# Two attention and gated layers on one core: a new instruction list for the input's stretch, and other step orders for six units

## The chip, the cores and the metric

The kernel runs on one core of one Trainium2 chip. The metric is the time of one execution on the device in microseconds (us). A core has five engines that run beside each other and wait for each other on semaphores: TensorE (PE in the profile, its weight loads PEld), VectorE (DVE), ScalarE (ACT), GpSimd (POOL) and SyncE (SP), which here only issues DMAs. Each engine works through its own instructions in the order in which the program wrote them, so a waiting instruction holds up all that stand behind it on its engine.

## The reference

The input x has 2048 rows of 448. Four sublayers follow each other, attention and a gated block in turn, twice over, with the same weights in both layers:

```python
x = x + A(layernorm(x)); x = x + B(layernorm(x))      # and both once more
# A: 16 heads of 28; q = h@wq for each head, one k = h@wk and one v = h@wv for all heads
#    softmax(q k^T * 28**-0.5) v, heads side by side, @ wo
# B: (sigmoid(h@w_gate) * (h@w_up)) @ w_down, inner width 1792
```

## The kernel before, in words

Everything is float32 in and out. Most products are done on float16 operands that are split in two: a high part (the rounded value) and a low part (the rest), so one product is three matmuls (high by high, high by low, low by high).

**The layer as units.** A layer is cut into 16 units of 128 rows, and a unit into 16 steps, one for each block of 128 keys, so a layer has 256 steps. One step does the scores of its unit's rows with its keys: four matmuls `s` (line 592), each followed by an exponential on ScalarE into a tile `P` (line 595), and, a step or so later, four products `pv` of `P` with the values (line 634, or 629 for halved tiles). Beside them a step computes row maxima of the unit after, since the exponent needs them: `Maxima.step` does one of 16 groups for a unit, four small matmuls `mx` (line 557) and four reductions on VectorE (line 562). After a unit's last group `row_max` reduces and rounds the maxima, and at the next visit of the maxima it transposes them on TensorE (`mt`, line 583), copies them (`mr`, line 585) and sends them by DMA into a row of the query tile `QS` (line 586): from GpSimd's queue for units 1 to 3, from SyncE's for the others. A unit's first scores can't start before that row has landed.

**The fill.** What is left, queries of later blocks (`qp`), the output projection (`wo`), the gated block (`gp`, `up`, `dn`), is handed out by `Filler.slice` in small pieces between the scores. How much a slice does follows from the work left over the steps left.

**The step orders.** The string for a step says in which order it writes its parts: S one score matmul with its exponential, F a slice of the fill, P the products of waiting steps, M one step of the maxima, X the stages that turn a finished unit into rows of the result (`tick`), and with it the pacing of the weights. `PATHS` has a pair of strings, for even and odd steps, and `pair_of` chooses the pair by layer and unit. `MORE` gives step 15 of unit 0 a second step of the maxima. Two steps of unit 1's maxima run before step 0.

**The input's stretch.** Before unit 0 stands a list written out by hand, `SEQ`. It takes x through statistics (s), normalization (n; last number 1: ScalarE, 0: VectorE), high part (g; 1: VectorE), low part (l; 1: GpSimd, 0: VectorE; lines 996 and 997), transposition on TensorE (t, line 338, and its copy, line 340), keys and values (k, line 355 `kv`), the keys' transposition (c, lines 396 and 397), the split of the query weights `WQ` (qs, qx, qy, qw), queries (f, slices of the fill), unit 0's 16 steps of the maxima (m), and dummy matmuls on the identity that keep TensorE's clock up (h, line 954). p is one step of the preparation of the other weights, e writes out what was put off.

**The weights.** `prep_b` reads the weights of the gated block and `wo`, takes their mean squares on ScalarE (line 109) for scales, and splits them, 46 splits in all. `HOWS` deals the splits: d is ScalarE and VectorE, p is ScalarE and GpSimd (lines 135 to 137), q is GpSimd alone (lines 141 to 143). `PLAN` says after how many steps of layer 0 how many steps of the preparation must be done. The split columns go to memory (line 254) and come back as `wgu` (line 769).

Of the kernel before, what the change touches and what calls it, by code (L numbers as in the profile page):

```python
# [19 lines left out]
def interleaved_layers_kernel(ctx: ExitStack, tc: tile.TileContext, x, wq, wk, wv, wo, wg, wu, wd, out, layers=2):  # L20
# [147 lines left out]
    def prep_b():  # L168
# [26 lines left out]
        def fetch(n):  # L195
            while todo and len(raw) < n:
                fn, *args = todo.pop(0)
                raw.append(fn(*args))
# [32 lines left out]
        for c in range(4):  # L231
            SPLIT[HOWS[c]](WO[:, 0, c], WO[:, 1, c], ro[c // 2][:, c % 2], swb[:, 0:1])
            fetch(c)
# [13 lines left out]
        for f in range(FC):  # L247
            r = get()
            st = big.tile([128, 2, 2, 4, 128], F16, tag="big", name="sgu")
            for j in (1, 0):  # L250
                SPLIT[HOWS[4 + 2 * f + j]](st[:, j, 0], st[:, j, 1], r[:, j], swb[:, 1 + j:2 + j])
                if j == 0:
# [6 lines left out]
        for f in range(0, FC, 2):  # L259
            r = get()  # L260
            for j in range(2):
                SPLIT[HOWS[32 + f + j]](WD[:, f + j, 0], WD[:, f + j, 1], r[:, j], swb[:, 3:4])
            yield
# [2 lines left out]


    SPLIT = {"d": split_d, "p": split_p, "q": split_pp}
    HOWS = "pppqdpppdqdqdqdppqdppqqqpdqpdpdqddpqqdqppdqdqd"
    PLAN = [(0, 9), (26, 29), (31, 33), (63, 61), (73, 67)]  # L270
    prepd = [0]

    def paced(step):

        k = next((i for i in range(len(PLAN) - 1) if PLAN[i + 1][0] > step), None)
        if k is None:
            n = 10 ** 6
        else:
            (a, p), (b, q) = PLAN[k], PLAN[k + 1]
            n = p + (q - p) * (step + 1 - a) / (b - a)  # L280
# [760 lines left out]
    def first_mx():  # L1041
# [8 lines left out]
          "h": heat, "a": lambda: next(pkv, None), "qs": qsq, "qx": qsum, "qy": lambda: next(pws), "qw": qsplit,  # L1050
          "q": queries, "f": lambda a: fill.slice(a * QCH / 100), "p": advance, "e": flush}
    SEQ = (
# [13 lines left out]
    )  # L1066
    for o in SEQ.split():
        a = o.split(",")
        DO[a[0]](*map(int, a[1:]))
    for b in range(1, NB):  # L1070
# [1 line left out]

    fill.slice(0.4 * QCH)
    early[0] = False
    MORE = (15,)
    HEAD = U * KT - 36
    sparse = ()
    PATHS = {
        "A": ("SFFFFSFFSSFPXM", "FSSFFSXPSM"),
        "A2": ("FFSFSSFSPXM", "FSFSFSSPMX"),  # L1080
        "B0": ("FSSFSXSPPM", "SFFSSFFXMFS"),
        "B1": ("FSFSFXSFSPMP", "SSFSFFXSFM"),
        "C": ("FFSXFSSSPPM", "SFFXMFFSSFSF"),
        "C2": ("FSXFSSSPPM", "SFFXFMSFSFS"),
        "C3": ("FSFSXFSSPPM", "SSFFFXSFFMS"),
        "D0": ("FSFSXFSSPPM", "FSFFSXSFFMS"),
        "D1": ("FSFSXFSSPPM", "FSFSFXSFSFM"),
        "E0": ("FFXFSSSSPPM", "SSFFFXSFFMS"),
        "E1": ("SFSFXFSSFPPM", "SSSFFXSM"),
    }  # L1090

    def pair_of(l, u):
        if not l and u < 4:
            return PATHS["A" if u < 2 else "A2"]
        if l and u < 3:
            return PATHS["C" if u < 2 else "C2"]
        if l and u == 3:
            return PATHS["C3"]
        return PATHS[("E" if l and u > 13 else "BD"[l]) + str(u % 2)]
# [4 lines left out]
    for l in range(layers):  # L1104
# [8 lines left out]
        else:  # L1113
            mx.todo.sort()
            n = sum(a[0] < 4 for a in mx.todo) + 4
# [10 lines left out]
        for step in range(U * KT):  # L1126
            u, kt = divmod(step, KT)
            if step == HEAD and not final:
                mxs[l + 1] = Maxima(l + 1)
            P = []  # L1130
            pair = pair_of(l, u)
            single = len(pair) == 2 and "P" in pair[0] and "P" in pair[1]
            for o in pair[kt % len(pair)]:
                if o == "S":
                    scores(l, u, kt, len(P), P)
                elif o == "M":
                    if l and step < 3 * KT:
                        n = step in sparse
                    else:
                        n = 1 + (u == 0 and kt in MORE)  # L1140
                    if not n:
                        mx.visit()
                    for _ in range(n):
                        if not mx.step() and not final and l + 1 in mxs:
                            a = mxs[l + 1].between()
# [28 lines left out]
        n = 0  # L1174
        nx = None if final else mxs[l + 1]
        while side or pend or (fill.gens if final else not nx.started()):
# [4 lines left out]
            a = None if final else nx.between()  # L1181
            if a:
# [7 lines left out]
                if go:  # L1190
                    nx.step(a)
                    n = 0
# [25 lines left out]
```

## Time and profile before

| what | value |
|---|---|
| time, median of 3 runs | 2234.21 us (2233.69 to 2234.92) |
| time of the profiled execution | 2234.31 us |
| its span in the profile | 2232.5 us |
| busy in the span: TensorE, VectorE, ScalarE, GpSimd | 2181.6, 1661.5, 1652.0, 910.0 us |
| granted TensorE clock, mean | 0.995 |
| first reduction of unit 0's maxima | 35.13 us |
| first scores of unit 0, 1, 2, 3 | 91.69, 145.82, 201.09, 260.01 us |

The span runs from the first instruction to the last; the rest of the execution's time lies around it. A busy TensorE is counted by matmuls that overlap each other, so a full row says that it had matmuls in it all the time, not that they ran at the highest rate. In a group's row the number after x is the count, then come busy us, the mean ns of one, and, behind the second bar, the idle time of the engine just before these instructions with what ended it.

### The profile page before, as it was taken

How to read it: one execution, taken by the hardware profiler on the slowest of the kernel's cores; microseconds unless marked ns; L12 is line 12 of the kernel's file. 1: busy time of each engine (PE TensorE's matmuls, PEld its weight loads, DVE VectorE, ACT ScalarE, POOL GpSimd, SP SyncE). 2: the span in 40 equal slices, each digit the busy share in tenths (PEclk: the TensorE clock that was granted, in tenths of full speed). 3: DMA queues.
4: the chain of work that ended last, by engine and by line, in shares of the span. 5: the costliest groups of instructions: out<-in, count | busy, mean ns of one | idle time of the engine just before them, and what ended most of it. 6: DMA issues, size and time to landing. Idle time of an engine off the chain costs nothing.

```text
span 2232.5 us, 43041 instructions
## 1 busy us (share of the span) xinstructions
PE 2181.6 (98%) x16306; PEld 1037.2 (46%) x16306; DVE 1661.5 (74%) x2983; ACT 1652.0 (74%) x2795; POOL 910.0 (41%) x1095
## 2 busy tenths in 40 slices
PE   7899999999999999999999999999999999999999
PEld 3322344454444444454564234545454545545467
DVE  7888877767767777777786556888888888888421
ACT  5698777776667777676623997888888888888851
POOL 4123775111111111111122011577676777767751
PEclk9999999999999999999999999999999999999999
DMA  5233662423223142332341113232231323232233
GB/s 175 74 96 87 204 212 75 121 62 114 89 62 112 39 125 73 105 100 60 113 151 54 36 52 101 70 108 80 87 94 53 105 62 103 62 108 78 97 109 116
DMA packets 203632, 213.39 MB, mean 96 GB/s; under 512 B 135376, under 2 KB 164240, under 8 KB 203424
## 3 DMA queue, kind: packets, MB, share of 16 engines
q1 hardware_dynamic: 198880, 195.88, 29.6%
q0 software_dynamic: 4544, 14.77, 1.7%
q8 instruction: 127, 2.08, 0.4%
q14 instruction: 81, 0.66, 0.1%
HBM read 175.37 MB, written 23.59 MB: 89 GB/s over the span
## 4 chain that ended last, share of the span: by engine, by line
PE 86%; DVE 5%; ACT 2%; DMA 1%; issue 1%; SPq 1%; POOL 1%; DVEq 0%; ACTq 0%; POOLq 0%
PE s L592 19%; PE pv L634 16%; PE dn L822 11%; PE gp L355 11%; PE up L355 11%; PE mx L557 7%; DVE mp L562 3%; PE wo L734 3%; PE pv L629 3%; PE qp L355 2%; ACT P L595 2%; DVE PH L611 1%; DMA sums<-rc 0%; SPq L453 0%; POOL PH L612 0%
## 5 line engine op out<-in xcount | busy, mean ns | idle before, releaser
L595 ACT ACTIVATE P<-s,esc 128x512 f32<-128x512 f32 x2048 | 1299.0, 693 | 356.2 <-PE s L592 336.7
L562 DVE TENSOR_REDUCE mp<-mx 128x1 f32<-128x512 f32 x2048 | 1269.8, 684 | 365.7 <-PE mx L557 360.9
L592 PE MATMUL s<-QS,KK 96*128 96x512 f16 x2048 | 694.9, 382 | 13.4 <-DVE mp L562 8.6
L355 PEld LDWEIGHTS <-wgu 128*128 128x128 f16 x4928 | 465.6, 97 | 200.2 <-issue 52.6
L612 POOL TENSOR_TENSOR PH<-P,PH 128x512 f16<-128x512 f32 x384 | 443.0, 1178 | 132.2 <-DVE PH L611 130.8
L634 PE MATMUL pv<-P,VV 128*32 128x512 f32 x3328 | 425.5, 601 | 0.0
L355 PE MATMUL gp<-XT,wgu 128*128 128x256 f16 x2464 | 357.1, 272 | 0.5 <-ACT P L595 0.2
L355 PE MATMUL up<-XT,wgu 128*128 128x256 f16 x2464 | 354.0, 273 | 3.5 <-DVE mp L562 3.5
L797 POOL TENSOR_TENSOR h<-th,h 128x512 f16<-128x512 f32 x112 | 130.9, 1168 | 454.4 <-ACT h L796 454.4
L822 PE MATMUL dn<-WD,h 128*128 128x448 f16 x1344 | 303.2, 352 | 0.0
L592 PEld LDWEIGHTS <-KK 96*128 96x128 f16 x2048 | 191.8, 97 | 210.6 <-issue 123.1
L557 PE MATMUL mx<-KK,QH 32*128 32x512 f16 x1792 | 187.8, 384 | 7.8 <-ACT P L595 4.5
L822 PEld LDWEIGHTS <-h 128*128 128x128 f16 x1344 | 126.6, 97 | 129.8 <-issue 13.0
L557 PEld LDWEIGHTS <-QH 32*128 32x128 f16 x1792 | 46.5, 91 | 250.5 <-issue 248.1
L634 PEld LDWEIGHTS pv<-P,VV 128*32 128x32 f32 x3328 | 81.9, 109 | 162.6 <-issue 141.8
L611 DVE CAST PH<-P 128x512 f16<-128x512 f32 x192 | 106.1, 578 | 31.8 <-ACT P L595 31.7
L309 POOL TENSOR_SCALAR rs<-mv 128x1 f32<-128x1 f32 (+1 forms) x50 | 13.4, 268 | 266.4 <-DVE mv L294 264.1
L796 ACT CAST h<-th 128x512 f16<-128x512 f32 x112 | 69.2, 618 | 61.9 <-DVE th L793 61.0
L355 PE MATMUL qp<-XT,WQ 128*128 128x512 f16 x352 | 109.3, 388 | 1.0 <-DVE mp L562 0.7
L609 ACT CAST PH<-P 128x512 f16<-128x512 f32 x192 | 110.2, 633 | 0.0
L793 DVE SCALAR_TENSOR_TENSOR th<-th,up 128x512 f32<-128x512 f32 x112 | 76.2, 681 | 39.1 <-PE up L355 37.7
L785 ACT ACTIVATE th<-gp,gsc 128x512 f32<-128x512 f32 x112 | 77.2, 689 | 33.4 <-PE gp L355 33.3
(166 smaller groups left out, 1188.0 us busy)
## 6 DMA issues: line engine op xcount, KB each, us to landing
wgu<-wgu_d SPq DMA_DIRECT2D x224, 512.0 KB
QS<-qd SPq DMA_DIRECT2D x384, 32.0 KB
lb<-sums SPq DMA_DIRECT2D x128, 64.0 KB
xr<-in_A_x_dram SPq DMA_DIRECT2D x32, 224.0 KB
qd<-qst POOLq DMA_DIRECT2D x28, 256.0 KB, 2.6
wgu_d<-sgu POOLq DMA_DIRECT2D x14, 512.0 KB, 4.0
x2d<-x SPq DMA_DIRECT2D x16, 224.0 KB
xr<-x2d SPq DMA_DIRECT2D x16, 224.0 KB
```

The lines of the kernel that those rows point to most:

```text
L355: nc.tensor.matmul(ps, a, b, start=n == 0, stop=n == 10)
L557: nc.tensor.matmul(ps[h][:, i * w:(i + 1) * w], qh[32 * h:32 * h + 32, g], KK[l][32 * h:32 * h + 32, 1, ka:kz], start=True, stop=True, til ...
L562: nc.vector.tensor_reduce(o, ps[h].rearrange("p (g k) -> p g k", g=n), axis=AX.X, op=OP.max)
L592: nc.tensor.matmul(s, KK[l][0:96, 0, kt * 128:(kt + 1) * 128], QS[l, u][:, g].rearrange("p h n -> p (h n)"), start=True, stop=True)
L595: nc.scalar.activation(p, s, AF.Exp, scale=esc)
L609: nc.scalar.copy(hi, p)
L611: (nc.vector if how == "d" else nc.gpsimd).tensor_copy(hi, p)
L612: nc.gpsimd.tensor_tensor(lo, p, hi, op=OP.subtract)
L634: nc.tensor.matmul(v[32 * g:32 * g + 32], VV[l][:, kt], P[g], start=kt == 0, stop=kt == KT - 1, tile_position=(0, 32 * g))
L785: defer(lambda: nc.scalar.activation(th, gp.rearrange("p j n -> p (j n)"), AF.Tanh, scale=gsc))
L797: nc.gpsimd.tensor_tensor(h[:, 1], t, h[:, 0], op=OP.subtract)
L822: nc.tensor.matmul(p, hs[f // 2][:, a, o:o + 128], WD[:, f, c], start=n == 0, stop=n == 3 * FC - 1)
```

## The change

Four tables are changed, and two lines of code that read them.

`SEQ` is another list with the same parts: 16 statistics, normalizations, high parts, low parts, transpositions, keys, 16 steps of the maxima, 136 dummy matmuls. Fifteen low parts go to GpSimd, where nine did; one stays on VectorE, where seven were. The scale of the query weights (qx, qy) is asked for ahead of the first transpositions, and no dummies stand ahead of the first scale. `PATHS` has a pair of its own for each of units 0 to 5 of layer 0 (A0 to A5), where units 0 and 1 shared A, 2 and 3 shared A2, and 4 and 5 had B0 and B1. The second step of the maxima in step 15 (`MORE`) is gone; `EXTRA` puts one more M into step 100 (unit 6). In layer 1 the odd string of C3 (unit 3) and of D0 (units 4, 6, 8, 10, 12) and both strings of E1 (unit 15) are reordered. `HOWS` deals the splits in another order: 15 d, 19 p, 12 q, where there were 15, 16 and 15. `PLAN` has its last point at (72, 66).

```diff
-    HOWS = "pppqdpppdqdqdqdppqdppqqqpdqpdpdqddpqqdqppdqdqd"
-    PLAN = [(0, 9), (26, 29), (31, 33), (63, 61), (73, 67)]
+    HOWS = "qppddqpppddqppdpdqdddqpqdpdpppdpqpqqdpdqpdqpqp"
+    PLAN = [(0, 9), (26, 29), (31, 33), (63, 61), (72, 66)]
...
-        "h,2 h,3 s,0,2,0 e s,2,4,0 r,0 f,20 a e h,18 e h,2 n,1,0 g,1,0 qs,1 r,2 a n,0,0 n,3,0 qs,3 g,3,0 "
-        "g,0,1 l,1,0 l,0,0 t,0,0 l,3,0 h,2 n,2,0 h,2 a h,1 e qs,0 e g,2,0 h,3 qs,2 l,2,1 f,30 t,1,0 p "
+        "e a s,0,2,0 h,2 r,0 h,3 h,2 h,18 s,2,4,0 e e qs,1 a n,1,0 e h,1 g,1,1 qs,0 h,2 qs,3 r,2 n,0,0 n,3,0 "
+        "h,3 f,5 l,1,1 n,2,0 g,3,1 g,0,0 l,0,1 l,3,1 qs,2 qx g,2,0 f,100 t,0,0 l,2,1 s,4,8,1 a t,1,0 t,2,0 e "
...
-    MORE = (15,)
+    EXTRA = {100: 5}
...
-        "A": ("SFFFFSFFSSFPXM", "FSSFFSXPSM"),
-        "A2": ("FFSFSSFSPXM", "FSFSFSSPMX"),
+        "A0": ("FSFFFSFFFSSPMX", "SSFFFSXPMS"),
+        "A1": ("FSFFSFFFSSPXM", "FFSFSFSFXPSM"),
+        "A2": ("SFFFFFFSFSFFFFFSFXPMFF", "FFSSPSFFSMXF"),
+        "A3": ("FFSSFSSPMX", "FSFFSSSPMX"),
+        "A4": ("SFFXSSSPPM", "SFFFSSFFXSFMFF"),
+        "A5": ("FXFSSSPMPS", "SFSFSXSFFFMFFF"),
...
-        "C3": ("FSFSXFSSPPM", "SSFFFXSFFMS"),
-        "D0": ("FSFSXFSSPPM", "FSFFSXSFFMS"),
+        "C3": ("FSFSXFSSPPM", "SSFFSFXSFFM"),
+        "D0": ("FSFSXFSSPPM", "FSFFSSXFFMFS"),
...
-        "E1": ("SFSFXFSSFPPM", "SSSFFXSM"),
+        "E1": ("SFSFXMFSSFPP", "FSSSFFXSM"),
...
-        if not l and u < 4:
-            return PATHS["A" if u < 2 else "A2"]
+        if not l and u < 6:
+            return PATHS["A" + str(u)]
...
-            for o in pair[kt % len(pair)]:
+            path = pair[kt % len(pair)]
+            if not l and step in EXTRA:
+                path = path[:EXTRA[step]] + "M" + path[EXTRA[step]:]
+            for o in path:
...
-                        n = 1 + (u == 0 and kt in MORE)
+                        n = 1
```

Three places show what this does to the engines' own orders.

GpSimd in the input's stretch, before, from its first square roots on (rs is a tile of row statistics, hl a tile's high and low parts, xr a tile of x, WQ the query weights, ro the raw `wo`):

```order
L971 TENSOR_TENSOR rs<-rs,mhalf 128x2 x2
L996 TENSOR_TENSOR hl_274<-xr_136,hl_274 128x64
L997 TENSOR_TENSOR hl_274<-xr_136,hl_274 128x384
L207 MEMSET ro 128x896 x2
L309 TENSOR_SCALAR rs<-mv 128x4
```

The same place now:

```order
L971 TENSOR_TENSOR rs<-rs,mhalf 128x2 x2
L996 TENSOR_TENSOR hl_234<-xr_128,hl_234 128x64
L997 TENSOR_TENSOR hl_234<-xr_128,hl_234 128x384
L996 TENSOR_TENSOR hl_256<-xr_126,hl_256 128x64
L997 TENSOR_TENSOR hl_256<-xr_126,hl_256 128x384
L996 TENSOR_TENSOR hl_254<-xr_138,hl_254 128x64
L997 TENSOR_TENSOR hl_254<-xr_138,hl_254 128x384
L996 TENSOR_TENSOR hl_267<-xr_136,hl_267 128x64
L997 TENSOR_TENSOR hl_267<-xr_136,hl_267 128x384
L309 TENSOR_SCALAR rs<-mv 128x4
```

The low parts of the first four tiles follow each other on GpSimd, ahead of the statistics of tiles 4 to 7, where tile 2's alone stood.

VectorE just ahead of the first reductions of unit 0's maxima, before (ktl is a block of keys, KK the transposed keys, mp the maxima):

```order
L389 SCALAR_TENSOR_TENSOR ktl_111<-kv,ktl_111 128x28
L991 CAST hl_519<-xr_147 128x448
L987 TENSOR_SCALAR xr_149<-xr_149,mv,rs 128x448
L996 TENSOR_TENSOR hl_519<-xr_147,hl_519 128x64
L997 TENSOR_TENSOR hl_519<-xr_147,hl_519 128x384
L400 COPY KK<-kvt 128x2x128
L562 TENSOR_REDUCE mp<-mx 128x1 x4
```

The same place now:

```order
L996 TENSOR_TENSOR hl_441<-xr_145,hl_441 128x64
L997 TENSOR_TENSOR hl_441<-xr_145,hl_441 128x384
L400 COPY KK<-kvt 128x2x128
L389 SCALAR_TENSOR_TENSOR ktl_111<-kv,ktl_111 128x28
L987 TENSOR_SCALAR xr_149<-xr_149,mv,rs 128x448
L562 TENSOR_REDUCE mp<-mx 128x1 x4
```

Tile 6's high and low parts (hl_519) have left VectorE; the low part that stays there is tile 5's (hl_441).

SyncE's queue of DMAs around the maxima of unit 5, before (rd is raw `w_down`, lb a row of sums, x2d the result of a unit, wgu split weights, XT a transposed tile):

```order
L192 DMA rd<-in_B_w_down_dram 128x2x448
L471 DMA QH<-qd_108 128x4x128
L586 DMA QS<-mr 1x16x128
L836 DMA x2d<-x_5103 128x448
L769 DMA wgu<-wgu_d 128x2048 x2
```

The same place now:

```order
L192 DMA rd<-in_B_w_down_dram 128x2x448
L471 DMA QH<-qd_108 128x4x128
L836 DMA x2d<-x_5073 128x448
L769 DMA wgu<-wgu_d 128x2048 x2
L586 DMA QS<-mr 1x16x128
```

The DMA of the maxima stands behind the store and the two loads. In steps: the transpose of the maxima of units 2 to 5 stood two steps ahead of the unit's first scores and stands one step ahead now; that of unit 1 stays at one.

23 rows, old and new, of the table SEQ are left out of this document.

## Prediction

> **What bounds the kernel now.** The profiled execution took 2234.31 us, its span is 2232.5, so 1.8 us lie around it; the median of the three runs is 2234.21, 0.1 less, and I use the profiled time for both. I first read busy time by stretch: the ramp up to the first row maxima, the stretch of unit 0's maxima, then units 0 to 4 and unit 6.
>
> ```profile
> 0.00:35.10 35.10, 26.06 (x186) 13.18 (x187) 23.88 (x88) 18.34 (x45) 12.56 (x23) 0.95 0.71 227
> 35.10:86.70 51.60, 43.13 (x383) 20.30 (x383) 47.21 (x97) 36.06 (x81) 17.66 (x35) 1.00 0.21 62
> 91.70:145.80 54.10, 50.34 (x291) 13.40 (x289) 45.29 (x84) 46.90 (x81) 14.87 (x14) 0.97 0.30 96
> 145.80:201.10 55.30, 52.44 (x304) 14.55 (x305) 46.92 (x89) 48.14 (x85) 6.37 (x13) 0.97 0.29 81
> 201.10:260.00 58.90, 53.67 (x314) 15.17 (x313) 49.70 (x83) 48.91 (x82) 42.80 (x42) 0.97 0.54 171
> 260.00:325.80 65.80, 63.74 (x463) 29.59 (x462) 49.98 (x85) 50.92 (x84) 50.06 (x48) 0.97 0.71 218
> 325.80:393.40 67.60, 65.54 (x456) 29.91 (x454) 52.81 (x90) 49.45 (x82) 38.52 (x40) 1.00 0.34 98
> 456.70:521.70 65.00, 65.00 (x465) 29.92 (x463) 47.20 (x84) 45.59 (x74) 10.40 (x19) 1.00 0.22 68
> ```
>
> The columns after the length are TensorE, weight loads, VectorE, ScalarE, GpSimd (busy us), granted clock, DMA share and GB/s. Unit 6 is full of matmuls (65.00 of 65.00); there only less matmul work could help, and the change removes none: both programs have the same number of each matmul, 136 dummies included. So whatever is won before unit 5 goes through to the end, and can come only from the ramp, the maxima, and the holes of units 0 to 4.
>
> The stretch of the maxima belongs to VectorE: 47.21 of 51.60 us, and GpSimd idles for two thirds of it. The groups there:
>
> ```profile
> L562 DVE TENSOR_REDUCE mp<-mx 128x1 f32<-128x512 f32 x64 | 39.3, 686 | 3.6 <-PE mx L557 3.6
> ...
> L400 DVE COPY KK<-kvt 128x256 f16<-128x256 f16 x2 | 0.6, 283 | 0.0
> L997 DVE TENSOR_TENSOR hl<-xr,hl 128x384 f16<-128x384 f32 x1 | 0.6, 551 | 0.0
> L991 DVE CAST hl<-xr 128x448 f16<-128x448 f32 x1 | 0.4, 385 | 0.0
> L996 DVE TENSOR_TENSOR hl<-xr,hl 128x64 f16<-128x64 f32 x1 | 0.2, 224 | 1.9 <-ACT hl L991 1.9
> ```
>
> 64 reductions at 0.6 us apiece (39.3/64) are fixed. What can go is the rest and the idle 4.4 us (51.60 - 47.21).
>
> In units 0 to 2 no engine is full: TensorE idles 3.8 + 2.9 + 5.2 = 11.9 us, VectorE 8.8 + 8.4 + 9.2, ScalarE 7.2 + 7.2 + 10.0. There the order of the steps decides.
>
> **The change, part by part.**
>
> *The ramp.* The first maxima wait for the query weights' split on VectorE and for two query chains on TensorE:
>
> ```profile
> 22.08 0.51 DVE L987 TENSOR_SCALAR xr<-xr,mv,rs 128x448 f32<-128x448 f32 x1
> 22.50 0.68 DVE L127 SCALAR_TENSOR_TENSOR WQ<-rq,swa,WQ 128x448 f16<-128x448 f32 x1
> 23.09 1.28 DVE L987 TENSOR_SCALAR xr<-xr,mv,rs 128x448 f32<-128x448 f32 x1
> ...
> 26.03 0.68 DVE L127 SCALAR_TENSOR_TENSOR WQ<-rq,swa,WQ 128x448 f16<-128x448 f32 x1
> ```
> ```profile
> 29.29 3.00 PE L355 MATMUL qp<-XT,WQ 128*128 128x512 f16 x11
> 32.13 0.22 PE L396 MATMUL kvt<-id,ktl 128*128 128x128 f16 x1
> 32.18 0.22 PE L397 MATMUL kvt<-id,ktl 128*128 128x128 f16 x1
> 32.24 2.54 PE L355 MATMUL qp<-XT,WQ 128*128 128x512 f16 x11
> 34.71 0.40 PE L557 MATMUL mx<-KK,QH 32*128 32x512 f16 x4
> ```
> ```profile
> 26.80:30.20 3.40, 3.40 (x28) 0.50 0.86 344
> ```
>
> The new list has 15 query matmuls ahead of the first maxima instead of 22: 7 x 0.23 us (2.54/11) = 1.6. It takes five low parts off VectorE ahead of them (six stood there, tile 5's stays). A low part there is L996 and L997, 0.22 + 0.55 less an overlap of some 0.15, 0.6 us; four of the five stand ahead of the weights' last split at 26.03, so that comes 4 x 0.6 = 2.4 earlier. Together -4.0. From above the bound is 0: the five go to GpSimd, where each is longer,
>
> ```profile
> L997 POOL TENSOR_TENSOR hl<-xr,hl 128x384 f16<-128x384 f32 x9 | 8.2, 914 | 0.0
> ...
> L996 POOL TENSOR_TENSOR hl<-xr,hl 128x64 f16<-128x64 f32 x9 | 2.8, 308 | 17.7 <-ACT hl L991 16.4 <-DVE hl L991 1.4
> ```
>
> 1.2 us, in one queue. Before, that queue stood still most of the ramp (12.56 of 35.10 busy), which is the cover; without it the transposes wait for the low parts. From below, -5.7: the window above shows the clock at 0.50 for 3.4 us after a hole on TensorE, and a fuller ramp could save those 1.7 us too. I take -4.0.
>
> *The stretch of the maxima.* One low part (0.6), a cast (0.3) and a copy of keys (0.2) leave VectorE: 1.1 us. Of the 4.4 idle I take a third, 1.4, because the 1.9 us wait ahead of L996 goes with its instruction, while new waits for keys may come. Sum -2.5, between 0 and -5.5.
>
> *No second maxima step in unit 0.* The extra step (`MORE`) moves to step 100, in unit 6. Its four reductions are 2.4 us of VectorE; unit 0 has VectorE at 45.29 of 54.10, so I count half, -1.2 (0 to -2.4). In unit 6 VectorE has 17.8 us free, which hides them.
>
> *The starts of units 1 to 6.* That step also kept the maxima three steps ahead. Now a unit's row maxima end so that their transpose (mt) stands one step ahead of the first scores that need them, where it was two in units 2 to 5. Unit 1 already works so:
>
> ```profile
> 140.49 0.22 PE L583 MATMUL mt<-id,m 128*16 128x128 f16 x1
> ...
> 141.88 0.55 POOL L586 DMA_DIRECT2D QS<-mr  x1
> ```
> ```profile
> 145.82 0.39 PE L592 MATMUL s<-QS,KK 96*128 96x512 f16 x1 [0.21 <-DVE mp L562]
> ```
> ```profile
> DMA to landing us min/median/max: 1.6/1.7/3.9
> ```
>
> From transpose to scores 5.3 us went by, and the row's DMA could land as late as 141.88 + 3.9 = 145.8: no slack. Without the extra step the last step of unit 0 is shorter by up to 2.4, so unit 1 may wait 2. In unit 3,
>
> ```profile
> 251.68 0.22 PE L583 MATMUL mt<-id,m 128*16 128x128 f16 x1
> ```
> ```profile
> 255.06 0.53 POOL L586 DMA_DIRECT2D QS<-mr  x1
> ```
> ```profile
> 260.01 0.38 PE L592 MATMUL s<-QS,KK 96*128 96x512 f16 x1
> ```
>
> the DMA stood 3.4 us behind weight splits in GpSimd's queue; of the 8.3 us from transpose to scores one step (58.90/16 = 3.7) goes, 4.6 are left, against 3.4 + 1.7 or more: a wait of about 1, at most 3. In unit 5 the maxima's DMA on SyncE's queue comes after a store and two 512 KB loads (it stood ahead of them): 0 to 3. The scores stand in TensorE's in-order queue, so everything there waits, and with it VectorE and ScalarE. I take +4 in all, bounds 0 and +10.
>
> *Own step orders in units 0 to 5.* Each pair of steps keeps its scores, pv and (nearly) its maxima; the slices of fill are shared out by count, so work moves only within steps. I take a third of the 11.9 us of TensorE's holes in units 0 to 2, -4. Nothing excludes a loss; the bounds are -10 (most of the holes) and +4 (the same third the other way).
>
> *Splits dealt anew.* Fifteen splits use VectorE before and after; three go from GpSimd alone to ScalarE with GpSimd. ScalarE has 10 us free in unit 2 and 14.9 in unit 3, which hides them; costed at 0. If it doesn't, three casts cost some 2 us.
>
> *Other orders in layer 1.* The stages there are as full as unit 6. -1 (-3 to +1).
>
> Sum: -4.0 - 2.5 - 1.2 + 4 - 4 - 1 = -8.7; 2234.3 - 8.7 = 2225.6 us.
>
> **The rivals.** (a) *All of it passes*: the maxima's DMAs land in time and the orders close most holes: -6.5 - 1.2 - 8 - 2 = -17.7, 2216.6. For it: landings had a median of 1.7. Against: unit 1's lack of slack. Chance 0.18.
>
> (b) *The starts of units eat it*: +10 at the starts, orders worth nothing: -6.5 - 1.2 + 10 - 1 = +1.3, 2235.6, or up to 3 less. For it: GpSimd is busy 42.80 of 58.90 in unit 2 and 50.06 of 65.80 in unit 3, just where its queue carries the maxima. Chance 0.15.
>
> (c) *GpSimd's queue becomes the ramp's bound* (the other side). The low parts of tiles 0 to 3 take 4 x 1.2 = 4.8 us in one row, and a weight split of about 2.6 stands ahead of tile 4's; its transposes stand ahead of the remaining query matmuls. If tile 4's low part ends after 29.3, where the query chains began, each us goes to the first maxima. At 3.5 us late: +3.5, no gain in the stretch, unit starts +4, orders +1: +8.5, 2242.8. Against: by the rows above GpSimd would end tile 4's at about 25 to 26. Chance 0.12.
>
> (d) *The two engines lock each other out.* At 23.09 VectorE's normalization took 1.28 us, where the one at 22.08 took 0.51, while GpSimd ran this:
>
> ```profile
> 23.08 1.05 POOL L137 TENSOR_TENSOR WQ<-rq,WQ 128x448 f16<-128x448 f32 x1
> ```
>
> That is 0.77 us for one meeting; if each of the five moved parts of the ramp meets such an instruction, 3.9 us of its 4.0 are gone: -4.8, 2229.5. The Trainium skill, page "SBUF — State Buffer", section "Who interferes with whom", has this as a rule: VectorE and GpSimd share one port pair as an exclusive lock, and VectorE instructions in a two-port mode or with two SBUF inputs wait for a whole GpSimd instruction, or the reverse. The one meeting above agrees. Against it here: the reductions read PSUM, and most of what VectorE does beside the moved parts is statistics. Chance 0.10.
>
> **How the numbers follow.** The forecast has 0.45. About 0.2% (4.5 us) is what a measurement of this kernel can tell from no change. Faster by more: the forecast's cases below 2229.8 (0.41), (a) and half of (d): 0.64. Within: (b), the rest of (d), the forecast's upper end: 0.20. Slower: (c) and (b)'s worst: 0.16. The range leaves out part of (c) and the best end of (a): 2214 to 2239.
>
> **What would show it.** Right: the first reduction near 31 instead of 35.1, the last of unit 0's maxima near 80, the first scores near 85; waits of 1 to 3 us on the maxima's DMA at the starts of units 1, 3 or 5; fewer TensorE holes in units 0 to 2; unit 6 as long as before. Wrong: first maxima at 34 or later (then (c) or (d)); starts of units with waits of 3 us and more (b); or a change in units 6 to 15 or in layer 1 of over 3 us, which I don't account for.

## The result

The kernel after takes 2221.41 us, the median of 6 runs (2218.33 to 2223.72), against 2233.95 (2232.57 to 2234.92, 6 runs): ratio 0.9944, 95% interval 0.9931 to 0.9957, 12.5 us less. That is faster by more than the 0.2% that can be told, inside the range, and 4.2 us under the forecast of 2225.6. Its profiled run took 2223.18 us with a span of 2221.4, 11.1 us less than the profiled run of before. From one unit's first scores to the next:

| stretch | before, us | after, us | difference |
|---|---|---|---|
| start to the first scores | 91.69 | 86.34 | -5.35 |
| unit 0 | 54.13 | 54.37 | +0.24 |
| unit 1 | 55.27 | 53.05 | -2.22 |
| unit 2 | 58.92 | 58.42 | -0.50 |
| unit 3 | 65.78 | 62.08 | -3.70 |
| units 4 and 5 | 130.89 | 129.90 | -0.99 |
| units 6 and 7 | 131.91 | 134.46 | +2.55 |
| units 8 to 15 and the change of layer | 633.52 | 632.58 | -0.94 |
| layer 1 | 1010.41 | 1010.18 | -0.23 |

The busy time by stretch, in the same columns as for the kernel before (length, TensorE, weight loads, VectorE, ScalarE, GpSimd, granted clock, DMA share, GB/s):

```profile
0.00:30.30 30.30, 21.75 (x178) 11.82 (x179) 22.49 (x77) 17.99 (x45) 18.21 (x33) 1.00 0.75 236
30.30:82.40 52.10, 48.22 (x400) 23.17 (x396) 46.98 (x94) 36.54 (x84) 19.77 (x38) 0.90 0.24 78
86.30:140.70 54.40, 50.63 (x288) 13.50 (x286) 46.06 (x85) 46.38 (x81) 12.36 (x12) 0.94 0.29 94
140.70:193.75 53.05, 50.10 (x300) 13.59 (x301) 44.17 (x84) 47.69 (x85) 6.12 (x12) 1.00 0.29 85
193.75:252.20 58.45, 54.51 (x321) 14.77 (x317) 51.18 (x88) 49.52 (x83) 41.05 (x42) 1.00 0.62 186
252.20:314.30 62.10, 60.98 (x458) 28.87 (x459) 48.76 (x83) 51.15 (x86) 37.81 (x39) 1.00 0.66 206
314.30:381.10 66.80, 65.61 (x461) 30.40 (x461) 50.53 (x89) 49.59 (x83) 45.58 (x48) 1.00 0.35 112
444.20:510.60 66.40, 65.36 (x460) 29.10 (x458) 49.58 (x87) 44.74 (x73) 9.48 (x19) 1.00 0.23 66
```

The ramp is 4.8 us shorter (30.3 against 35.1) and its clock whole. The stretch of the maxima is no shorter (52.10 against 51.60) though VectorE has no more to do in it: the granted clock there is 0.90. From the last reduction to the first scores of unit 0 it takes 3.83 us instead of 4.99, in every trace with the new list; the prediction has no term for that. In unit 0 the clock is 0.94, in units 1 to 3 it is 1.00 where it was 0.97. So some of what the table gives to the orders is the clock: ahead of unit 6, half clock came five times for 3.4 us before (one in the ramp, one in each of units 0 to 3), and after in two stretches of 10.2 and 6.8 us, one in the maxima, one in unit 0. Both sum to 17 us. The two profiles may be compared as wholes, but not unit by unit. TensorE's holes in units 0 to 2 are 10.7 us (3.8 + 2.9 + 3.9) where they were 11.9.

The starts of units 1 and 3 on TensorE, and the answer for the line that issues the row's DMA:

```profile
140.71 0.39 PE L592 MATMUL s<-QS,KK 96*128 96x512 f16 x1 [1.30 <-DMA QS<-mr]
```
```profile
252.17 0.60 PE L592 MATMUL s<-QS,KK 96*128 96x512 f16 x2 [1.43 <-DMA QS<-mr]
```
```profile
DMA to landing us min/median/max: 1.6/1.7/4.0
```

The waits that I expected in units 1 and 3 are there, in the size expected, and there is none at the start of unit 5; what they cost is another question.

### The profile page after: what moved, and what is told of

It reads as the page before. It is cut to its first block, busy times and chain, and to the rows that moved or that the text cites. A ratio compares the mean times of both kernels' runs of the same rounds, so it can differ in the third digit from the quotient of the medians.

```text
span 2221.4 us, 43054 instructions
## 1 busy us (share of the span) xinstructions
PE 2177.6 (98%) x16306; PEld 1036.2 (47%) x16306; DVE 1662.4 (75%) x2969; ACT 1643.9 (74%) x2800; POOL 907.4 (41%) x1104
## 4 chain that ended last, share of the span: by engine, by line
PE 83%; DVE 8%; ACT 3%; issue 2%; DMA 2%; POOL 1%; SPq 1%; DVEq 0%; POOLq 0%; ACTq 0%
PE s L592 18%; PE pv L634 15%; PE up L355 12%; PE gp L355 11%; PE dn L822 11%; PE mx L557 7%; DVE mp L562 5%; PE wo L734 3%; PE pv L629 3%; PE qp L355 2%; ACT P L595 2%; DVE PH L611 1%; PE kv L355 0%; DMA QS<-mr 0%; DVE oT L715 0%
## 5 line engine op out<-in xcount | busy, mean ns | idle before, releaser
L592 PE MATMUL s<-QS,KK 96*128 96x512 f16 x2048 | 687.4, 381 | 15.8 <-DVE mp L562 6.9
```

The lines of the kernel that those rows point to most:

```text
L592: nc.tensor.matmul(s, KK[l][0:96, 0, kt * 128:(kt + 1) * 128], QS[l, u][:, g].rearrange("p h n -> p (h n)"), start=True, stop=True)
```

## The experiments

Times are medians with their range. The kernels ran in turns with the kernel before, four to a chip; across chips, ratios to it are compared. The kernel before had there a median of 2232.16 us for the first four, 2233.61 for the second four and 2231.74 for the last four; the kernel after, run again with the second four, took 2217.39.

**The list alone.** The kernel before with the new `SEQ`, with no other edit:

```diff
-        "h,2 h,3 s,0,2,0 e s,2,4,0 r,0 f,20 a e h,18 e h,2 n,1,0 g,1,0 qs,1 r,2 a n,0,0 n,3,0 qs,3 g,3,0 "
+        "e a s,0,2,0 h,2 r,0 h,3 h,2 h,18 s,2,4,0 e e qs,1 a n,1,0 e h,1 g,1,1 qs,0 h,2 qs,3 r,2 n,0,0 n,3,0 "
...
```

> The kernel before with the new list of the input's stretch alone (low parts of six tiles on GpSimd among it); step orders, the second maxima step of unit 0, splits and layer 1 as before. Theory (two separate gains, the opening some 5 us and the step orders some 7, less 3 at the starts of units): first reduction near 30.4, first scores of unit 0 near 86.5, and 4 to 6 us under the kernel before at the end, 2228 to 2230. Rival 1 (the list carries nearly all of the gain, units 1 to 4 only follow from it): 2221 to 2224. Rival 2 (the early start is given back in units 1 to 4 unless their orders change too): first scores 5 us earlier, but the end within 1.5 us of the kernel before.

2224.2 us (2222.08 to 2227.07), ratio 0.9963 (0.9951 to 0.9975): 8.0 us less, first scores at 84.2. More than the 4 to 6 of the theory, and the early start is not given back.

**The orders alone.** The other way round: the kernel after with the old list, deal and layer 1, so that only these stay of the change, beside the step moved from `MORE` to `EXTRA`:

```diff
+        "A0": ("FSFFFSFFFSSPMX", "SSFFFSXPMS"),
+        "A1": ("FSFFSFFFSSPXM", "FFSFSFSFXPSM"),
+        "A2": ("SFFFFFFSFSFFFFFSFXPMFF", "FFSSPSFFSMXF"),
+        "A3": ("FFSSFSSPMX", "FSFFSSSPMX"),
+        "A4": ("SFFXSSSPPM", "SFFFSSFFXSFMFF"),
+        "A5": ("FXFSSSPMPS", "SFSFSXSFFFMFFF"),
```

> The kernel after with the old list, the old splits' deal and the old orders of layer 1: against the kernel before, only the own step orders of units 0 to 5 and the extra maxima step moved from unit 0 to unit 6. Theory: first scores of unit 0 at 91.7 as before, units 1 to 4 some 7 us shorter in sum, 2226 to 2228. Rival 1 (the list carries nearly all): 2232 to 2235. Rival 2 (the orders work only with the new list, since the state that unit 0 begins with differs): slower than before by over 1 us, and the two parts measured alone add up to much less than 12.5.

2240.0 us (2236.98 to 2241.02), ratio 1.0031 (1.0019 to 1.0043): 7.8 us *slower*. Units 0 to 3 are together 6.9 us shorter than before (with 3.4 us at half clock in them, where it was 13.6, which may be most of it), but unit 4 takes 77.0 us where it took 67.6. The sign is the second rival's; its reason is not, as the run of the old deal shows.

**The low parts.** The kernel after with the low parts of six tiles on VectorE, each in its new place (`l,i,1` becomes `l,i,0` for tiles 0, 1, 3, 4, 6 and 13):

> The kernel after with the low parts of tiles 0, 1, 3, 4, 6 and 13 on VectorE again, in the new list's places. Theory by my term (four of them stand ahead of the weights' last split, 0.6 us each): first reduction 2.4 us later, near 32.8, and 2 to 3.5 us slower than the kernel after, 2223.5 to 2225. Rival (the order of the list and its fewer query matmuls did it, VectorE had idle time in the ramp that the low parts fit in): first reduction within 0.6 us of 30.4 and the end within 1 us of the kernel after.

2220.34 us (2217.87 to 2224.38), ratio 0.9945 (0.9932 to 0.9957), where the kernel after had 0.9944. The first reduction starts at 30.58 against 30.36. The engine of the low parts makes no difference; the rival holds. Why my 2.4 us are not there is seen at the weights' last split, first in the kernel after, VectorE and then GpSimd:

```profile
22.09 1.27 DVE L127 SCALAR_TENSOR_TENSOR WQ<-rq,swa,WQ 128x448 f16<-128x448 f32 x2
...
24.73 1.30 DVE L127 SCALAR_TENSOR_TENSOR WQ<-rq,swa,WQ 128x448 f16<-128x448 f32 x1
```
```profile
24.64 0.91 POOL L997 TENSOR_TENSOR hl<-xr,hl 128x384 f16<-128x384 f32 x1
```

and with the low part on VectorE, ahead of the split:

```profile
25.49 0.55 DVE L997 TENSOR_TENSOR hl<-xr,hl 128x384 f16<-128x384 f32 x1
25.96 0.67 DVE L127 SCALAR_TENSOR_TENSOR WQ<-rq,swa,WQ 128x448 f16<-128x448 f32 x1
```

The split takes 0.67 us undisturbed and 1.30 beside GpSimd's low part (1.30 to 1.31 in every other trace of the new list with the part there). What VectorE no longer does for this part it loses again by waiting: 0.63 us, the 0.6 that the part costs on VectorE itself. That is rival (d) at this place. The rule of the Trainium skill (page "SBUF — State Buffer", section "Who interferes with whom") that the two engines hold a port pair in turns, for whole instructions, agrees with these 1.30 us. The three low parts ahead of this one shift VectorE's splits before it by 0.6 us (22.09 against 22.71), not by 1.8; where the rest went was not traced.

So what shortened the ramp? TensorE in the kernel before, and then after, ahead of the first maxima:

```profile
25.70 0.23 PE L338 MATMUL t<-id,hl 128*128 128x128 f16 x1 [2.12 <-DVE hl L996]
26.17 0.34 PE L338 MATMUL t<-id,hl 128*128 128x128 f16 x3 [0.24 <-DVE hl L997]
```
```profile
23.67 1.67 PE L355 MATMUL qp<-XT,WQ 128*128 128x512 f16 x7
...
26.94 0.23 PE L396 MATMUL kvt<-id,ktl 128*128 128x128 f16 x1 [0.99 <-DVE ktl L389]
...
28.00 1.89 PE L355 MATMUL qp<-XT,WQ 128*128 128x512 f16 x8
...
29.93 0.39 PE L557 MATMUL mx<-KK,QH 32*128 32x512 f16 x4
```

Before, all 22 query matmuls stood behind transposes that waited 2.12 + 0.24 us for a low part. The new list puts 7 matmuls ahead of that place and 8 behind it, and the longest wait left is 0.99. So 1.4 us of waiting, 1.6 us for seven matmuls, and half clock that came after the hole (3.4 us, up to 1.7) come to 4.7 of the 4.8. It is the list's order and its seven fewer matmuls that did it, not the engine of the low parts; the three shares are read from the rows and were not tried apart.

**The row's queue.** The kernel after with all row DMAs on SyncE's queue:

```diff
-            (nc.gpsimd if 0 < u < 4 else nc.sync).dma_start(QS[l, u][28:29].rearrange("o g h n -> o (g h) n"), r)
+            nc.sync.dma_start(QS[l, u][28:29].rearrange("o g h n -> o (g h) n"), r)
```

> The kernel after with the row maxima's DMA of units 1 to 3 issued from SyncE's queue instead of GpSimd's, as the other units have it. Theory (TensorE waits 1.3 and 1.4 us on that row at the starts of units 1 and 3, and what is lost there goes through to the end): no such wait, 1.5 to 2.7 us faster than the kernel after, 2218.7 to 2220. Rival 1 (TensorE's wait is cover for VectorE or ScalarE, which are late themselves; the unit ends no sooner): within 1 us of the kernel after. Rival 2 (SyncE's queue holds loads and stores ahead of the row, which then lands later): waits of over 2 us at those starts, and 1 us slower or more.

2218.09 us (2216.97 to 2221.34), ratio 0.9938 (0.9927 to 0.9950); against the 0.9944 and 0.9928 of the kernel after this is no difference. The waits are gone. In the kernel after they change from trace to trace: 1.30 and 1.43 us in its first profile, 0.13 and 0.86 when it was run again. Units 0 to 3, which hold both, do not simply follow them. Less half of the time at half clock in them (an estimate of what it cost), they take 222.6 us here without waits, 222.8 in the kernel after run again and 224.5 in its first profile. Units 2 and 3 of this kernel, and then of the kernel after run again:

```profile
191.80:247.90 56.10, 54.14 (x320) 14.74 (x317) 49.49 (x85) 49.02 (x83) 40.88 (x41) 1.00 0.62 193
247.90:311.30 63.40, 61.21 (x458) 28.81 (x457) 50.23 (x86) 51.63 (x86) 37.75 (x39) 1.00 0.68 210
```
```profile
191.60:249.30 57.70, 54.54 (x321) 14.76 (x317) 50.61 (x87) 49.60 (x83) 41.09 (x42) 1.00 0.63 188
249.30:311.00 61.70, 60.93 (x457) 28.84 (x458) 49.23 (x84) 51.19 (x85) 37.81 (x39) 1.00 0.67 207
```

What unit 2 wins, unit 3 gives back. Its steps last the same to 0.05 us in both but for the sixth and seventh: 5.96 and 4.53 us here, 5.45 and 3.39 there. In the sixth VectorE waits for a row of sums (`rc`), and the reductions of the maxima stand behind that. The DMA of the sums comes in SyncE's queue behind twelve loads of query parts (VectorE, SyncE's queue and ScalarE here; VectorE in the kernel after run again, where the queue has the same order):

```profile
268.00 0.25 DVE L691 RECIPROCAL rc<-rc 128x16 f32<-128x16 f32 x1 [3.83 <-DMA rc<-sums]
```
```profile
257.33 8.79 SPq L453 DMA_DIRECT2D QS<-qd  x12
266.16 0.43 SPq L686 DMA_DIRECT2D rc<-sums  x1
```
```profile
271.76 0.72 ACT L135 ACTIVATE sgu<-rgu,swb 128x512 f16<-128x512 f32 x1 [1.17 <-DMA rgu<-in_B_w_up_dram]
```
```profile
268.24 0.25 DVE L691 RECIPROCAL rc<-rc 128x16 f32<-128x16 f32 x1 [2.73 <-DMA rc<-sums]
```

The sums come at the same moment in both, 268.0 and 268.2, though the unit began 1.3 us earlier here; then, in the seventh step, ScalarE's split waits 1.17 us for raw weights, which it does not in the kernel after. So a wait at the start of this unit can be cover for the later wait for the sums; that is read from the rows, and no run moved the DMA of the sums. With the old orders it stands ahead of the twelve loads, and VectorE does not wait for it there.

**The old deal.** The kernel after with the splits dealt as before:

```diff
-    HOWS = "qppddqpppddqppdpdqdddqpqdpdpppdpqpqqdpdqpdqpqp"
-    PLAN = [(0, 9), (26, 29), (31, 33), (63, 61), (72, 66)]
+    HOWS = "pppqdpppdqdqdqdppqdppqqqpdqpdpdqddpqqdqppdqdqd"
+    PLAN = [(0, 9), (26, 29), (31, 33), (63, 61), (73, 67)]
```

> The kernel after with the old deal of the weights' splits and the old plan of their steps, nothing else. Theory (the new orders of units 3 and 4 need the new deal: with the old one two splits of VectorE stand ahead of a maxima step at the start of unit 4, TensorE waits for VectorE and its clock is halved behind the hole, as in the orders alone, where unit 4 took 77.0 us): unit 4 near 77 instead of 66.9, 8 to 10 us slower than the kernel after. Rival 1 (my term: ScalarE's idle time hides what the deal moves): within 2 us of the kernel after. Rival 2 (the slow unit 4 came from the old list, by which loads of the down weights come at other times): unit 4 near 67, within 2 us.

2231.06 us (2226.91 to 2234.76, 11 runs), ratio 0.9991 (0.9980 to 1.0001): 13.7 us slower than the kernel after beside it, no run of the one among those of the other. In the profiles it is 8.4 (spans of 2226.4 and 2218.0): the profiled run was one of the fastest of the eleven, which go up to 2234.76 where the granted clock was 0.993 instead of 0.998. With the new orders, nearly the whole gain hangs on the deal. Unit 4 here (near 74, not the 77 of the theory) and in the kernel after run again:

```profile
311.70:385.60 73.90, 68.65 (x461) 30.95 (x461) 53.70 (x92) 50.10 (x83) 37.75 (x41) 0.98 0.32 102
```
```profile
311.00:377.90 66.90, 65.69 (x462) 30.49 (x462) 50.61 (x89) 49.69 (x83) 45.70 (x48) 1.00 0.35 113
```

And where it begins, VectorE, TensorE and ScalarE with the old deal:

```profile
311.51 2.48 DVE L562 TENSOR_REDUCE mp<-mx 128x1 f32<-128x512 f32 x4
313.91 2.11 DVE L131 SCALAR_TENSOR_TENSOR WD<-rd,swb,WD 128x448 f16<-128x448 f32 x2
315.94 2.47 DVE L562 TENSOR_REDUCE mp<-mx 128x1 f32<-128x512 f32 x4
```
```profile
316.67 0.37 PE L557 MATMUL mx<-KK,QH 32*128 32x512 f16 x1 [2.01 <-DVE mp L562]
```
```profile
315.64 0.67 ACT L135 ACTIVATE WD<-rd,swb 128x448 f16<-128x448 f32 x1 [1.93 <-DMA rd<-in_B_w_down_dram]
```

Two VectorE splits stand between two maxima steps, so TensorE, which needs the reductions to free its `mx` tiles, waits 2.01 us; and a split on ScalarE, there ahead of its load, holds up the exponentials behind it for 1.93. With the new deal no VectorE split stands there, and ScalarE's split does not wait. That makes the first two steps of unit 4 3.8 us longer. Another 3.0 are in the ninth and tenth: a VectorE split stands between two maxima steps there too, and half clock follows for 3.4 us. Units 2 and 3 are longer as well, by 1.4 and 1.6 us. The list alone had the old deal with the old orders, and unit 4 took 67.5: it is the new orders that need the new deal. Whether the letters or the plan's last point does it was not tried.

**The lead.** The kernel after with the second maxima step in the last step of unit 0 again:

```diff
-    EXTRA = {100: 5}
+    EXTRA = {}
+    MORE = (15,)
...
-                        n = 1
+                        n = 1 + (u == 0 and kt in MORE)
```

> The kernel after with the second maxima step in the last step of unit 0 again and none in unit 6, so that the transposes of the row maxima stand a step earlier in units 2 to 5. Theory (the starts of units wait for the row's DMA, and the step moved to unit 6 is not hidden there: units 6 and 7 took 134.5 us after and 131.9 in every program with the step in unit 0): no wait at the starts of units 2 and 3, units 6 and 7 near 132, unit 0 longer by up to 2.4; 2 to 4 us faster than the kernel after. Rival 1 (the step in unit 0 costs more there than it gives, VectorE being busy 0.85 of unit 0): within 1 us of the kernel after or slower. Rival 2 (unit 3's own order was made for the shorter lead, its gain of 3.7 us goes): 2 us slower or more.

2220.38 us (2218.51 to 2223.61), ratio 0.9945 (0.9932 to 0.9958): 3.0 us slower than the kernel after by the medians, with ranges that overlap, and not faster; the first rival holds. Unit 0 here, and in the kernel after:

```profile
84.70:139.60 54.90, 51.71 (x292) 13.82 (x291) 46.57 (x86) 45.93 (x81) 12.37 (x12) 0.94 0.29 95
```
```profile
86.50:138.30 51.80, 49.00 (x288) 13.26 (x286) 44.78 (x83) 45.28 (x80) 12.38 (x12) 0.97 0.29 94
```

3.1 us longer; half clock lasts 6.8 us here and 3.4 there, by estimate 1.7 of the 3.1, so about 1.4 is the step itself. The waits at the starts are gone (0.13 and 0.86 there), but units 1 to 3 take 172.2 us against 172.7. Unit 6 is only 0.6 us shorter, unit 7 the same, so the longer units 6 and 7 are not mainly the moved step.

**The clock.** What ate the gain in the stretch of the maxima? The kernel after, the three microseconds ahead of each half-clock stretch and what follows:

```profile
45.30:48.40 3.10, 1.59 (x20) 0.63 (x19) 2.81 (x8) 3.10 (x7) 2.28 (x7) 1.00 0.61 169
48.40:51.80 3.40, 3.20 (x20) 1.26 (x21) 3.40 (x7) 2.38 (x6) 2.46 (x5) 0.50 0.41 91
...
86.30:89.40 3.10, 1.94 (x7) 0.48 (x6) 2.96 (x8) 2.61 (x5) 0.00 (x0) 1.00 0.31 69
89.40:92.80 3.40, 3.29 (x14) 0.77 (x13) 2.45 (x5) 1.95 (x3) 0.84 (x1) 0.50 0.66 180
```

TensorE is 51% and 63% busy in them, its longest hole 0.82 us. So ten dummies were put into the holes:

```diff
-        "g,10,0 f,14 s,12,16,2 t,9,0 f,50 f,20 h,2 m n,11,1 e k,8 e f,60 m f,10 g,11,0 n,12,1 e c,8,0 f,9 m "
+        "g,10,0 f,14 s,12,16,2 t,9,0 f,50 f,20 h,2 m n,11,1 e h,3 k,8 e f,60 m f,10 g,11,0 n,12,1 e h,3 c,8,0 f,9 m "
...
                     scores(l, u, kt, len(P), P)
+                    if not l and not step:
+                        heat(1)
```

> The kernel after with ten more dummy matmuls: three ahead of the keys of tile 8 and three ahead of the key transposes of tile 8, where TensorE stood idle 0.8 us each, and one behind each scores matmul of unit 0's first step. Theory (a stretch of about 3 us in which TensorE is busy for two thirds or less is followed by half clock for 3.4 us or a multiple; that took what the shorter list gave in the stretch of the maxima): clock 1.00 from 45 to 96 us where it was 0.50 for 10.2 and 6.8 us, first scores of unit 0 some 3 us earlier and 3 to 6 us faster than the kernel after. Rival 1 (half clock comes whatever the holes are): the same 17 us of it, within 1 us or 1 us slower by the dummies' own time. Rival 2 (the stretch is VectorE's; TensorE's clock is hidden behind it): the clock holds, but the end is within 1 us.

> The kernel after as it is, on the same chip as the other three, so that they can be set against it: 12 us faster than the kernel before, as it was (ratio 0.9944).

2215.66 us (2212.82 to 2217.23), ratio 0.9921 (0.9907 to 0.9936); the kernel after beside it 2217.39 (2215.25 to 2219.76), 0.9928 (0.9914 to 0.9941). The same places with the dummies:

```profile
47.00:50.00 3.00, 2.61 (x13) 0.60 (x10) 2.97 (x6) 2.96 (x8) 2.58 (x10) 1.00 0.64 190
50.00:53.00 3.00, 2.33 (x29) 1.33 (x29) 3.00 (x6) 2.19 (x6) 0.88 (x3) 1.00 0.22 47
...
82.90:86.00 3.10, 2.52 (x11) 0.81 (x10) 2.96 (x8) 2.52 (x5) 0.00 (x0) 1.00 0.27 59
86.00:89.00 3.00, 2.98 (x20) 0.89 (x20) 2.62 (x5) 1.85 (x3) 0.84 (x1) 1.00 0.56 148
```

No half clock is left in the first 460 us. The first reduction starts at 30.28, the last of unit 0's 64 ends at 79.02: 48.7 us, where it was 52.2 after and 51.6 before. First scores come 3.6 us earlier and units 6 and on 5.6 earlier than in the profile of the kernel after beside it. By the profiles this is worth 4 us; by the medians 1.7, with overlapping intervals, since the unprofiled runs of the kernel after had a better clock (0.997 to 0.999) than the profiled one (0.996). The theory's 3 to 6 us are met by the profiles, not by the medians. In the traces with the new list the length of the stretch follows the half clock in it: 48.7 us with none, 50.1 with 3.4 us, 51.2 with 6.8 and 52.2 to 52.8 with 10.2. That the clock was held and the stretch shortened is shown; how much it is worth at the end is not settled. When this kernel was run again, the clock held there too, but 3.4 us of half clock came in unit 3, behind a wait of 2.28 us for the row.

**With the clock held.** The last four start from that kernel, run again as control. `held_sync` has the row's DMA on SyncE, as above; `held_old_orders` and `held_shared_4_5` read:

```diff
-        if not l and u < 6:
-            return PATHS["A" + str(u)]
+        if not l and u < 4:
+            return PATHS["A" if u < 2 else "A2"]
```

(the old orders in units 0 to 5, with the old `"A"` and `"A2"`), and

```diff
-        if not l and u < 6:
+        if not l and u < 4:
```

(own orders in units 0 to 3 alone).

> The kernel after with the ten more dummy matmuls, as it was, as the control of the other three: clock 1.00 from 45 to 96 us, 0.9921 of the kernel before, 2214 to 2217.

> The control with the row maxima's DMA of units 1 to 3 issued from SyncE's queue. Theory as it now stands (TensorE's waits for the row are real, but units 1 to 3 together take as long without them: 173.1 us with the row by SyncE, 172.7 with it by GpSimd): within 1 us of the control. Rival (that pair differed by its clock and by the unlucky DMA landings of one run; the waits count): 1.5 to 2.7 us faster than the control, and units 1 to 3 shorter by as much.

> The control with the old step orders of units 0 to 5 (two shared pairs for units 0 to 3, the common pair for units 4 and 5); the new list, the new deal of splits and the place of the extra maxima step stay. Theory (the own orders are worth 3 to 5 us, nearly all of it in unit 3, 61.7 us against 65.8 to 66.9 with the old order): unit 3 near 65.5, 3 to 5 us slower than the control. Rival 1 (the new deal makes unit 3 short by itself, since it changes which engine splits there): unit 3 near 62, within 1 us. Rival 2 (what units 0 to 3 lose, units 4 to 7 give back, since their orders lengthen units 6 and 7): unit 3 longer, but within 1.5 us at the end.

> The control with the old common order in units 4 and 5; units 0 to 3 keep their own. Theory (units 4 to 7 took 264.4 us with own orders in 4 and 5, against 262.8 with the common one in the list alone; the loss shows in units 6 and 7, behind the orders that cause it): units 6 and 7 near 131.9 instead of 134.5, 1.5 us faster than the control. Rival 1 (the new deal was made for the own orders, the common order with it waits at the weights' splits of unit 4): unit 4 above 69, 2 us slower or more. Rival 2 (units 6 and 7 are longer by the maxima step that moved there): units 6 and 7 still at 134.5, within 1 us.

| kernel | median, us (range) | ratio to before (interval) |
|---|---|---|
| control | 2216.06 (2215.59 to 2217.23) | 0.9932 (0.9920 to 0.9945) |
| row by SyncE | 2217.25 (2216.04 to 2218.70) | 0.9937 (0.9925 to 0.9950) |
| old orders | 2219.15 (2218.36 to 2223.17) | 0.9949 (0.9937 to 0.9962) |
| shared order in units 4 and 5 | 2216.09 (2214.62 to 2218.95) | 0.9936 (0.9922 to 0.9950) |

The row by SyncE wins nothing again: less half of the time at half clock, units 0 to 3 take 224.9 us with it, against 222.7 in the control, whose waits at the starts are 0.51 and 2.28 us. The old orders cost 3.1 us by the medians, and no run of theirs is among the control's; by the profiles it is 1.1 (spans of 2216.4 and 2215.3). Units 0 to 3 with the old orders, and in the control:

```profile
82.60:134.80 52.20, 48.82 (x292) 13.21 (x290) 45.67 (x84) 47.07 (x81) 12.39 (x12) 1.00 0.31 98
134.80:190.10 55.30, 52.57 (x303) 14.21 (x304) 44.75 (x86) 48.16 (x85) 6.46 (x13) 0.97 0.29 83
190.10:248.20 58.10, 52.43 (x315) 14.94 (x314) 50.28 (x86) 49.51 (x83) 40.62 (x42) 1.00 0.59 185
248.20:311.30 63.10, 61.65 (x462) 29.07 (x463) 51.22 (x84) 52.64 (x86) 40.84 (x41) 1.00 0.64 208
```
```profile
82.80:133.30 50.50, 48.20 (x293) 13.46 (x292) 45.20 (x83) 45.59 (x81) 12.37 (x12) 1.00 0.30 100
133.30:186.40 53.10, 50.16 (x301) 13.62 (x302) 44.93 (x86) 48.16 (x86) 6.13 (x12) 1.00 0.30 87
186.40:245.10 58.70, 54.37 (x321) 14.62 (x317) 52.00 (x88) 49.53 (x83) 41.41 (x43) 1.00 0.64 185
245.10:307.20 62.10, 61.95 (x457) 28.95 (x458) 47.88 (x82) 51.46 (x85) 37.51 (x39) 0.97 0.64 206
```

They are 4.2 us longer (52.2 + 55.3 + 58.1 + 63.1 = 228.7 against 224.4), with half clock once in each, in unit 1 and in unit 3, so that up to 1.7 us of what these two units differ by is the clock. The gain is not nearly all in unit 3, as the theory had it: unit 0, at full clock in both, has 1.7 of it. Unit 3 took 65.8 and 66.9 us with the old order, the old deal and 3.4 and 6.8 us at half clock; with the old order and the new deal it takes 63.1. So the deal or the clock made most of the 3.7 us that the first table has there. Units 4 to 7 give 2.7 us back: 261.7 against 264.4. The shared order in units 4 and 5 shows one source: with it units 6 and 7 take 132.9 us instead of 134.5, but units 4 and 5 take 0.4 more, and at the end there is no difference. No version is shown to beat the control.

## Why the prediction came out right, term by term

**The ramp (-4.0): right in size, wrong in the working.** It measured -4.8. The step that failed is "four of the five stand ahead of the weights' last split at 26.03, so that comes 4 x 0.6 = 2.4 earlier": the split ends at 26.03 + 0.68 before and 24.73 + 1.30 = 26.03 after, 0.7 earlier, and the low parts alone bring 0.2 at the first reduction. Rival (d), with a chance of 0.10, took just this gain. That the size fits is luck. In its place stood a wait of TensorE that I had not read, 2.12 us for a low part at 25.70.

**The stretch of the maxima (-2.5): right, and hidden.** With the clock held it is 48.7 us against 51.6, -2.9. In the profile after it is +0.5, since 10.2 us of it ran at half clock. I had the clock in the ramp's bounds only, not in the stretch. The 1.2 us between the last reduction and the first scores come on top, without a term.

**No second maxima step in unit 0 (-1.2): right, as far as is known.** Putting it back costs unit 0 about 1.4 us beside the clock, by estimate, and the kernel 3.0 by medians whose ranges overlap.

**The starts (+4): the step that failed most.** Waits of 1.30 and 1.43 us came in units 1 and 3 as forecast, and none in unit 5. The two together are 1.0 to 2.8 us in the traces of the kernel after and of the control, so even charged in full they fall short of 4. And taking them away, in three kernels and two ways, won nothing at the end that could be told. I charged a wait on TensorE's path in full ("everything there waits") without asking what sets the pace of the unit that it opens; in unit 3, by the rows above, that is a later wait for a row of sums. Whether some of the wait's price is left, and the row on SyncE's queue costs as much elsewhere, the runs do not tell. About +4 became about 0. That is near the size by which the forecast was too slow; that the other misses (the stretch's clock and units 6 and 7 on one side, the ramp, the 1.2 us behind the maxima and the undisturbed units on the other) come near to cancelling is luck.

**The orders (-4) and the deal (0): right only together.** The orders are worth 3.1 us with the new deal, by the medians; with the clock held, TensorE's holes in units 0 to 2 are 9.6 us with them and 11.8 without, 2.2 less and not 4. With the new orders and the old deal the kernel loses 13.7. My "ScalarE has 10 us free in unit 2 and 14.9 in unit 3, which hides them" asked which engine has time to spare; what counted was what stands between two maxima steps in VectorE's queue, and in which unit. The price "some 2 us" was a seventh of what it is by the medians.

**Unit 6 as long as before: wrong.** Units 6 and 7 are 2.55 us longer. The shared order in units 4 and 5 takes 1.6 of it away and the step put back in unit 0 takes 0.6, each by itself.

**Layer 1 (-1): no more than that.** From its unit 4 to 14 it is 1.0 to 1.3 us shorter in every kernel with the new orders (619.8 to 620.1 us against 621.1), but its first four units and its last two give most of that back: layer 1 as a whole is 0.2 us shorter in the profile.

The median lies halfway between the forecast (2225.6) and rival (a) (2216.6): the starts cost nothing that could be told, as (a) had it, but the orders closed fewer holes than it asked.

## What to carry to other kernels

A wait at the head of a stretch can be cover for a later one: look for a wait further on that ends at the same moment either way, and charge the first only beyond it. When an instruction is moved from VectorE to GpSimd, look what VectorE does beside it there. A new order and a new deal of engine work are one edit: price them together, by what stands between the instructions that others wait for.

## What the runs showed of the hardware

- TensorE's clock halves though TensorE never stands still for long: it was busy 1.59 of 3.10 us, no hole over 0.82, ahead of 10.2 us at half clock. The half-clock stretches last 3.4, 6.8 or 10.2 us in all traces here, but for the one that each trace ends in. The Trainium skill (page "TensorE: Matmul & The Clock Gate", section "Part 1: The HAM clock gate (the "warmup" mystery)") has windows of about 3.4 us and a cold clock after an idle one; the lengths agree, but here a window half busy was enough.
- Not every stretch as idle as that halves the clock: with the old deal TensorE was busy 0.86 of the 3.10 us from 314.2, and the clock stayed whole. In each trace the half-clock stretches begin whole multiples of 3.413 us apart (before at 26.83, 95.09, 146.29, 235.04 and 289.65 us: 20, 15, 26 and 16 of them). Counted in windows on that grid (the fourteen traces, 17 to 470 us, by the records of the matmuls), half clock followed all 5 windows in which TensorE was busy for half or less, 20 of 58 with 51 to 72%, and none of 1741 with more. So a hole that falls across two windows can pass.
- Most of the spread from run to run is this clock: run beside the experiments, the kernel before took 2228.7 to 2229.9 us in its four runs at a mean granted clock of 0.997, and 2233.1 to 2236.4 in its eight at 0.994 and 0.993.
- The same split on VectorE takes 0.67 us alone and 1.30 beside a GpSimd instruction of 0.91.
- Issued from GpSimd, the row's DMA of units 1 and 3 landed after some 4 us in the kernel after (136.87 to 140.66 and 248.09 to 252.13), where the median of the six that GpSimd issues there is 1.7. In the other traces these two took 1.6 to 4.9.
